# One K tile of the third head split into parts of 64, 48, 8, 4 and 4 partitions

## The chip, the core and the metric

The kernel runs on one core of a Trainium2 chip. The time is the device time of one execution in microseconds (us), lower is better. Before the change it is 177.32 us, the median of three runs (177.17 to 178.05). The core has five instruction streams that matter here: PE (matrix products), DVE (vector work, here mostly 32 x 32 transposes), ACT, POOL, and SP, which in this kernel does nothing but issue transfers. The transfers themselves are carried out by 16 DMA engines. Each transfer is divided among them by rows, each engine works through its own queue in order, and each reports to the transfer's semaphore when its share is done; the transfer is complete when all have.

## The reference

Two rounds of attention and a gated block, each with a residual connection, for four sequences with one new position each:

```python
x = x + _A_ref(_layernorm(x), A_k_cache, A_v_cache, A_wq, A_wo)
x = x + _B_ref(_layernorm(x), B_w_gate, B_w_up, B_w_down)
x = x + _A_ref(_layernorm(x), A_k_cache, A_v_cache, A_wq, A_wo)
x = x + _B_ref(_layernorm(x), B_w_gate, B_w_up, B_w_down)
```

`_A_ref` makes 32 query heads from x, takes the last W = 2048 positions of the K and V caches (8 key heads of width 128, each shared by four query heads), forms softmax(q k / sqrt(128)) v and multiplies by wo. `_B_ref` is (sigmoid(x w_gate) * (x w_up)) w_down with an inner width of 1792. All data are bf16. Both attention rounds read the same caches and weights, with another x.

## The kernel before

All data come through SBUF from HBM. An arena of 50 slots, 4 KB per partition each, holds tiles; most tiles are two slots, 128 partitions of 8 KB, 1 MB. The K tiles of all eight heads take 32 slots and stay from the first round to the second, so K is loaded once. V, wq, wo and the weights of the gated block go through the remaining 18 slots and a side buffer, and most of V and all of wq are loaded a second time for the second round.

One K tile holds one head and two of the four sequences. `pair_d` (line 478) gives its source: for each of 64 row groups p and each of the two sequences b, one run of 32 positions, 8 KB. Row p of sequence b lands in partition 2p + b. `kpair(h, bp)` (line 482) is the tile for head h and sequence pair bp: slots 4h + 2bp and the one after it. `load_k` (line 485) issues the two tiles of a head. Its first three heads (`AHEAD = 3`) are issued at the start, behind the four wq tiles; from there on a list of loads (lines 1478 to 1502) gives the order: K3, wo of the first two heads, V0, K4, V1, K5 and so on. The loads are on SP in exactly that order.

For head h, `k_transpose` (line 885) transposes the four slots in place on DVE: T{h}_0 and T{h}_1 in the two slots of tile (h, 0), T{h}_2 and T{h}_3 in those of tile (h, 1). `softmax_unit` (line 896) then makes the scores on PE (line 918, behind the mask's products at line 907), the maximum on DVE (line 931) and the exponentials on ACT (line 946); `turn_p` (line 957) permutes and transposes the result, `pv_unit` (line 995) multiplies with the two V tiles (line 1009), and `wo_unit` with wo. A V tile's slot goes back to the pool after its products, and the next load that is waiting on SP takes it. The front of head h + 2 is written down ahead of the PV products of head h. The very last weights are the three w_down tiles of the second gated block; their products are line 1428, and a copy (line 1439) and a transfer of 4 KB out end the kernel.

No engine runs the operations in the order in which they are written. Each is noted with an engine, an estimated duration, and the tokens that it reads and writes (`_Plan.op`, line 52); a planner (`_schedule`, line 92) walks all of them with estimated times, transfers included, and gives each engine but SP a fixed order, earliest possible start first. SP keeps the order as written. `_assign_sync` (line 180) then adds the semaphore waits that the tokens require. There are 24 semaphores for transfers; each transfer uses the next, and waits until the transfer 24 places before it has landed.

A token `("slot", n)` stands for one slot; `tok(s)` is the pair of a tile. Everything that reads a slot waits for the last operation that wrote its token.

Of the kernel before, what the change touches and what calls it, by code (L numbers as in the profile page):

```python
# [254 lines left out]
class _SlotPool:  # L255
# [16 lines left out]
    bw_8k=421.0, bw_4k=409.0, bw_3k=405.0, bw_1k=347.0,  # L272
# [6 lines left out]
def build(nc, A_x, A_k, A_v, A_wq, A_wo, B_wg, B_wu, B_wd, out, cfg=None):  # L279
# [29 lines left out]
    AHEAD = 3  # L309
# [15 lines left out]
    with es:  # L325
# [52 lines left out]
        def slot_ap(s):  # L378
            if s == SIDE:
                return side[:, 0:SLOT]  # L380
            return arena[:, s * SLOT:(s + 1) * SLOT]
# [4 lines left out]
        def tile_ap(s):  # L386
            return arena[:, s * SLOT:(s + 2) * SLOT]

        def tok(s):
            return [("slot", s), ("slot", s + 1)]  # L390

        def c_dve(n, rate=None):
            return tm["dve_fix"] + n * (tm["dve_f32"] if rate is None else rate)
# [4 lines left out]
        def dma(name, dst, src, w, r=(), rate="bw_4k", nbytes=None, sem=None):  # L398
            if nbytes is None:
                nbytes = dst.partition_size() * dst.free_nbytes()  # L400
            o = P.op("sync", name, 0.0, lambda e, dst=dst, src=src: e.dma_start(dst, src),  # L401
                     r=r, w=w, dma_bytes=nbytes, dma_rate=tm[rate])
            if sem is not None:
                o.sem = sem
                o.inc = 16
            return o
# [56 lines left out]
        def need(name):  # L463
            while name not in where:
                take_load()
            return where[name]
# [11 lines left out]
        def pair_d(cache, h, bp):  # L478

            return cache[2 * bp:2 * bp + 2, h, SK - W:SK, :].rearrange("b (p j) d -> p b (j d)", p=64)  # L480

        def kpair(h, bp):
            return tile_ap(4 * h + 2 * bp)

        def load_k(h):
            where[("K", h)] = h
            for bp in range(2):
                dma("K%d_%d" % (h, bp), kpair(h, bp), pair_d(A_k, h, bp), w=tok(4 * h + 2 * bp), rate="bw_8k")

        def load_half(name, src, rate, size, where_):  # L490
            left[name] = 1
            homes[name] = [where_]
            on_free[name] = lambda s: hfree.add(s)

            def emit(s):
                dma(str(name), slot_ap(s)[:, 0:size], src, w=stok(s, size), rate=rate)
            loads.append((name, emit))
# [134 lines left out]
        def keep_wq(c):  # L632
            def f(s):
# [13 lines left out]
             r=[("ones_f",)], w=[("e", 0)])  # L647
# [6 lines left out]
        for jh in range(2):  # L654
            for bp in range(2):
                for i in range(2):
# [7 lines left out]
                         r=[("ones_f",), ("e", 0), ("perm",)], w=[("perm", jh, bp, i)])  # L664
# [5 lines left out]
             r=[("ones_f",), ("e", 0)], w=[("msk_s",)])  # L670
        P.op("vector", "msk_s2", 100.0, lambda v: v.tensor_scalar(msk_s[:, :], msk_s[:, :], -1.0e30, None, ALU.mult),
             r=[("msk_s",)], w=[("msk_s",)])
        P.op("gpsimd", "msk_m", 200.0,
             lambda g: g.affine_select(msk_m[:, :], ones_f[:, 0:2], [[-1, 2]], ALU.is_equal, 0.0, base=0, channel_multiplier=1),
             r=[("ones_f",), ("e", 0)], w=[("msk_m",)])
        P.op("vector", "sel_f", 200.0,
             lambda v: v.tensor_reduce(sel_f[:, :], perm[:, :].rearrange("p (g x) -> p x g", x=NR), AXX, ALU.add),
             r=perms + [("e", 0)], w=[("sel_f",)])
        P.op("gpsimd", "sel_b", 200.0, lambda g: g.tensor_copy(sel_b[:, :], sel_f[:, :]),
             r=[("sel_f",), ("e", 0)], w=[("sel_b",)])  # L680
        P.op("vector", "sel_r", 100.0,
             lambda v: v.tensor_reduce(sel_r[:, :], sel_f[:, :].rearrange("p (g y) -> p y g", g=2), AXX, ALU.add),
             r=[("sel_f",), ("e", 0)], w=[("sel_r",)])
        P.op("vector", "eyew", 200.0,
             lambda v: v.tensor_reduce(eyew[:, 96:128], ident.rearrange("p (a j) -> p j a", a=4), AXX, ALU.max),
             r=[("e", 0), ("eyew0",)], w=[("eyew",)])
        P.op("vector", "maskp", 200.0,
             lambda v: v.tensor_reduce(maskp[:, :], ident.rearrange("p (a j) -> p a j", a=4), AXX, ALU.max),
             r=[("e", 0)], w=[("maskp",)])
        P.op("vector", "maskb", 100.0,  # L690
             lambda v: v.tensor_reduce(maskb[:, :], maskp[:, :].rearrange("p (j b) -> p b j", j=2), AXX, ALU.max),
             r=[("maskp",)], w=[("maskb",)])
# [3 lines left out]
             r=[("eyew",)], w=[("maske",)])  # L696
        P.op("vector", "mod4", 100.0,
             lambda v: v.tensor_reduce(mod4[:, :], ey.rearrange("p (e m) -> p m e", m=REP), AXX, ALU.max),
             r=[("eyew",)], w=[("mod4",)])
# [4 lines left out]
             r=[("mod4",), ("maskp",)], w=[("selm",)])  # L704
# [4 lines left out]
             r=[("e", 0)], w=[("permo",)])  # L709
# [4 lines left out]
             r=[("sel_r",)], w=[("maskr",)])  # L714
# [170 lines left out]
        def k_transpose(h):  # L885
            need(("K", h))
            for t in range(4):
                v32 = slot_ap(4 * h + t).bitcast(F32)
                P.op("vector", "T%d_%d" % (h, t), c_dve(1024), lambda v, v32=v32: v.transpose(v32, v32),  # L889
                     r=[("slot", 4 * h + t)], w=[("slot", 4 * h + t)])  # L890

        ucount = [0]

# [314 lines left out]
        def attn_first():  # L1208
            def front(h):
                k_transpose(h)  # L1210
                softmax_unit("0.%d" % h, h)
                turn = lambda: turn_p(0, "0.%d" % h, h % 2, PBS[h % 2])
                return turn
# [265 lines left out]
        for h in range(AHEAD):  # L1479
            loads.append((("K", h), lambda _, h=h: load_k(h)))  # L1480
        for h in range(HKV):
            if h + AHEAD < HKV:
                loads.append((("K", h + AHEAD), lambda _, h=h + AHEAD: load_k(h)))
            if h % 2 == 0 and h + 2 < HKV:
                load_wo(h // 2)
            for bp in range(2):
                load_v(h, bp, 0, 2 if (h, bp) in keep + stay else 1)
# [21 lines left out]
        n = len(P.ops)  # L1509
# [45 lines left out]
def bass_interleave_layers__sliding_block_cached__glu_gated_glu__decode_kernel(  # L1555
    nc, A_x, A_k_cache, A_v_cache, A_wq, A_wo, B_x, B_w_gate, B_w_up, B_w_down, out,
):
    build(nc, A_x, A_k_cache, A_v_cache, A_wq, A_wo, B_w_gate, B_w_up, B_w_down, out)
# [28 lines left out]
```

## Time and profile before

| | |
|---|---|
| median of three runs | 177.32 us (177.17 to 178.05) |
| the profiled execution's own time | 177.11 us |
| its span, first to last instruction | 175.4 us |
| data moved by transfers (queue q1) | 69.74 MB in 12344 packets |
| PE busy | 107.5 us, 61% of the span |
| DVE busy | 104.5 us, 60% |
| K tiles: issue to landing, median | 24.9 us |
| V tiles of 1 MB: issue to landing, median | 16.5 us |

The page of the profile has the DMA engines' mean busy share in tenths for 40 equal slices of the span, the queues with their packets, and the chain of waits that ended last. The queues q8 and q14 are instruction fetches: the engines' programs are read through the same 16 DMA engines as the data. "Chain" lines give the start, the length and what was running or waited for. Time line rows give start, length, engine, line, operation, output and input, shapes and a count, with the idle time just before in brackets and what ended it. Besides these views the trace keeps, for every transfer, the times at which its semaphore was counted up, and for every packet its start, length and size; times read from there are given with the transfer they belong to.

In SP's order the transfers that matter are numbered: 1 to 4 wq, 5 and 6 K0, 7 and 8 K1, 9 and 10 K2, 11 and 12 K3, 13 wo, 14 and 15 V0, and 81 to 83 the last three w_down tiles.

### The profile page before, as it was taken

How to read it: one execution, taken by the hardware profiler on the slowest of the kernel's cores; microseconds unless marked ns; L12 is line 12 of the kernel's file. 1: busy time of each engine (PE TensorE's matmuls, PEld its weight loads, DVE VectorE, ACT ScalarE, POOL GpSimd, SP SyncE). 2: the span in 40 equal slices, each digit the busy share in tenths (PEclk: the TensorE clock that was granted, in tenths of full speed). 3: DMA queues.
4: the chain of work that ended last, by engine and by line, in shares of the span. 5: the costliest groups of instructions: out<-in, count | busy, mean ns of one | idle time of the engine just before them, and what ended most of it. 6: DMA issues, size and time to landing. Idle time of an engine off the chain costs nothing.

```text
span 175.4 us, 3934 instructions
## 1 busy us (share of the span) xinstructions
PE 107.5 (61%) x1663; PEld 55.4 (32%) x1663; DVE 104.5 (60%) x258; ACT 32.7 (19%) x87; POOL 22.1 (13%) x90
## 2 busy tenths in 40 slices
PE   0536246259566273561766456558977999776584
PEld 0203112014334041340445452143222444425432
DVE  6307997994957738378322382315399999733351
ACT  2002021322303003021030000100133455430011
POOL 6100010101101001010010000000011553442000
PEclk9999999999999999999999999999999999965555
DMA  5999999999999999999999999999999999999980
GB/s 177 422 430 428 420 422 422 409 419 420 422 422 409 422 422 422 419 407 424 424 405 423 415 397 406 405 406 403 409 411 404 422 422 422 420 415 419 419 347 28
DMA packets 12370, 70.00 MB, mean 399 GB/s; under 512 B 1336, under 2 KB 1344, under 8 KB 6336
## 3 DMA queue, kind: packets, MB, share of 16 engines
q1 hardware_dynamic: 12344, 69.74, 97.2%
q8 instruction: 13, 0.21, 0.5%
q14 instruction: 5, 0.04, 0.1%
q10 hardware_dynamic: 8, 0.00, 0.0%
HBM read 69.73 MB, written 0.00 MB: 398 GB/s over the span
## 4 chain that ended last, share of the span: by engine, by line
DMA 71%; PE 12%; DVE 8%; SPq 6%; issue 1%; DVEq 0%
DMA arena<-in_A_v_cache_dram 48%; DMA arena<-in_B_w_down_dram 15%; SPq L401 6%; DMA arena<-in_A_wq_dram 4%; DMA arena<-in_B_w_up_dram 4%; PE ps L1009 3%; PE ps L918 2%; PE ps L1092 2%; DVE arena L592 1%; DVE small L931 1%; PE ps L1383 1%; DVE ps L599 1%; PE ps L907 1%; PE ps L959 1%; PE ps L1428 1%
## 5 line engine op out<-in xcount | busy, mean ns | idle before, releaser
L889 DVE STREAM_TRANSPOSE arena<-arena 128x1024 f32<-128x1024 f32 x32 | 37.0, 1204 | 0.1
L1009 PE MATMUL ps<-side,arena 128*128 128x8 bf16 x576 | 18.2, 168 | 13.8 <-DMA arena<-in_A_v_cache_dram 13.8
L918 PE MATMUL ps<-arena,side 128*32 128x512 bf16 x256 | 25.1, 525 | 0.0
L1009 PEld LDWEIGHTS ps<-side,arena 128*128 128x128 bf16 x576 | 16.8, 104 | 20.1 <-DMA arena<-in_A_v_cache_dram 18.4
L931 DVE TENSOR_REDUCE small<-ps 128x1 f32<-128x512 f32 x16 | 10.8, 676 | 17.3 <-PE ps L918 17.2
L946 ACT ACTIVATE side<-ps,small 128x512 bf16<-128x512 f32 x16 | 11.0, 687 | 36.9 <-PE ps L1028 18.4
L907 PE MATMUL ps<-small,msk_s 128*32 128x512 bf16 x64 | 8.6, 526 | 14.1 <-DVE arena L889 13.3
L882 ACT CAST side<-ps 128x256 bf16<-128x256 f32 x16 | 5.9, 371 | 34.3 <-PE ps L918 25.6
L961 ACT CAST side<-ps 128x512 bf16<-128x512 f32 x16 | 9.4, 586 | 10.8 <-PE ps L959 10.8
L918 PEld LDWEIGHTS ps<-arena,side 128*32 128x32 bf16 x256 | 8.1, 119 | 10.2 <-issue 7.2
L975 POOL CAST small<-small 128x1 bf16<-128x1 f32 x9 | 1.7, 187 | 76.2 <-ACT side L946 76.2
L959 PE MATMUL ps<-side,perm 128*128 128x512 bf16 x16 | 8.1, 507 | 5.0 <-ACT side L946 5.0
L830 PE MATMUL ps<-arena,xn 128*4 128x512 bf16 x60 | 7.6, 574 | 3.4 <-DMA arena<-in_A_wq_dram 3.2
L786 ACT ACTIVATE small<-ps 128x4 f32<-128x4 f32 x4 | 0.7, 174 | 48.2 <-PE ps L782 48.2
L1383 PE MATMUL ps<-arena,xn 128*4 128x448 bf16 x60 | 7.0, 550 | 3.1 <-DMA arena<-in_B_w_up_dram 1.5
L1092 PE MATMUL ps<-arena,side 128*32 128x512 bf16 x112 | 8.2, 416 | 0.2 <-DVE small L943 0.2
L966 DVE STREAM_TRANSPOSE side<-side 128x256 f32<-128x256 f32 x16 | 6.9, 432 | 2.2 <-ACT side L961 2.0
L877 PE MATMUL ps<-side,eyew 32*128 32x64 bf16 x64 | 5.6, 217 | 3.3 <-ACT side L882 2.4
L907 PEld LDWEIGHTS ps<-small,msk_s 128*32 128x32 bf16 x64 | 1.7, 98 | 17.0 <-DVE arena L889 15.6
L1018 DVE TENSOR_TENSOR onb<-ps,rinv 128x16 bf16<-128x16 f32 x9 | 1.7, 185 | 9.0 <-PE ps L1009 8.8
L842 DVE STREAM_TRANSPOSE side<-ps 128x512 f32<-128x512 f32 x3 | 2.1, 717 | 7.9 <-PE ps L830 7.8
L1392 DVE STREAM_TRANSPOSE side<-ps 128x448 f32<-128x448 f32 x4 | 2.6, 640 | 7.0 <-PE ps L1383 7.0
(126 smaller groups left out, 139.5 us busy)
## 6 DMA issues: line engine op xcount, KB each, us to landing
arena<-in_A_v_cache_dram SPq DMA_DIRECT2D x26, 1024.0 KB, 16.5
arena<-in_A_k_cache_dram SPq DMA_DIRECT2D x16, 1024.0 KB, 24.9
arena<-in_A_wq_dram SPq DMA_DIRECT2D x4, 1024.0 KB, 7.9
arena<-in_A_wo_dram SPq DMA_DIRECT2D x3, 1024.0 KB, 26.6
arena<-in_A_v_cache_dram SPq DMA_DIRECT2D x6, 512.0 KB, 6.8
arena<-in_A_wq_dram SPq DMA_DIRECT2D x5, 512.0 KB, 6.6
arena<-in_B_w_up_dram SPq DMA_DIRECT2D x4, 448.0 KB, 6.1
arena<-in_B_w_gate_dram SPq DMA_DIRECT2D x2, 896.0 KB, 20.8
```

Of the source, the lines that this page charges most:

```text
L401: o = P.op("sync", name, 0.0, lambda e, dst=dst, src=src: e.dma_start(dst, src), r=r, w=w, dma_bytes=nbytes, dma_rate=tm[rate])
L830: last = pe.matmul(ps[32 * hh:32 * hh + NB, qb, :], xn[:, c * NB:(c + 1) * NB], src[:, o + hh * 512:o + (hh + 1) * 512], start=(c == 0), s ...
L889: P.op("vector", "T%d_%d" % (h, t), c_dve(1024), lambda v, v32=v32: v.transpose(v32, v32), r=[("slot", 4 * h + t)], w=[("slot", 4 * h + t)])
L907: last = pe.matmul(ps[32 * gi:32 * gi + 32, bank, :], msk_s[:, :], msk_m[:, :].unsqueeze(1).broadcast_to([128, 256, 2]), start=True, stop= ...
L918: last = pe.matmul(ps[32 * gi:32 * gi + 32, bank, :], qbd[:, q0:q0 + 32], kt[:, cp // 2, cp % 2, jh * NJ:(jh + 1) * NJ, :], start=False, s ...
L931: lambda v: v.tensor_reduce(nmax[:, k2:k2 + 1], ps[:, bank, :], AXX, ALU.max),
L946: lambda a: a.activation(prow[:, :].rearrange("p (m x t) -> p m x t", x=32, t=2), ps[:, bank, :].rearrange("p (m t x) -> p m x t", x=32, t ...
L959: lambda pe: pe.matmul(ps[:, pb, :], perm[:, :], prow[:, :], start=True, stop=True),
L961: P.op("scalar", "pc" + tag, c_act(512), lambda a: a.copy(prow[:, :], ps[:, pb, :]), r=[("ppb", pb)], w=[("prow",)], banks=(pb,))
L1009: last = pe.matmul(ps[:, ob, bp * 8:bp * 8 + 8], slot_ap(ss[j // NJ])[:, j % NJ * 128:(j % NJ + 1) * 128], ev[:, j % 2, j % 16 // 2, x0:x0 ...
L1092: last = pe.matmul(ps[32 * g:32 * g + 32, ob, :], ew[:, g, mq, t], src.rearrange("p (m t d) -> p t m d", t=2, d=128)[:, t], start=(n == 0) ...
L1383: last = pe.matmul(ps[32 * g:32 * g + NB, gub[n], 0:NF], xn[:, c * NB:(c + 1) * NB], src[:, g * NF:(g + 1) * NF], start=(c == 0), stop=(c ...
```

## The change

The tile of head 2 and sequences 0 and 1 (`CUT = AHEAD - 1 = 2`, bp = 0) is no longer one transfer. Part 0 is all 64 rows of sequence 0 (partitions 0, 2, ..., 126). Part 1 is rows 0 to 47 of sequence 1 (partitions 1, 3, ..., 95). Both stand in the old place. The last 16 rows of sequence 1 follow: rows 48, 50, ..., 62 (partitions 97, 101, ..., 125) behind the other tile of head 2, rows 49, 53, 57, 61 (partitions 99, 107, 115, 123) behind the first tile of head 3, rows 51, 55, 59, 63 (partitions 103, 111, 119, 127) behind its second tile. Part 0 carries the slots' own tokens; parts 1 to 4 have tokens of their own, `("rows", 1)` to `("rows", 4)`, and the transposes T2_0 and T2_1 read all four. SP's order at the start becomes wq, K0, K1, part 0, part 1, K2_1, part 2, K3_0, part 3, K3_1, part 4, wo, V0.

```diff
+        CUT = AHEAD - 1
+
+        def k_rows(n):
+            b, p0, p1, step = ((0, 0, 64, 1), (1, 0, 48, 1), (1, 48, 64, 2), (1, 49, 64, 4), (1, 51, 64, 4))[n]
+            dma("K%dr%d" % (CUT, n), kpair(CUT, 0)[2 * p0 + b:128:2 * step, :] if p1 == 64 else kpair(CUT, 0)[2 * p0 + b:2 * p1:2 * step, :],
+                pair_d(A_k, CUT, 0)[p0:p1:step, b, :], w=[("rows", n)] if n else tok(4 * CUT), rate="bw_8k")
+
         def load_k(h):
             where[("K", h)] = h
             for bp in range(2):
+                if (h, bp) == (CUT, 0):
+                    k_rows(0)
+                    k_rows(1)
+                    continue
                 dma("K%d_%d" % (h, bp), kpair(h, bp), pair_d(A_k, h, bp), w=tok(4 * h + 2 * bp), rate="bw_8k")
+                if h == CUT:
+                    k_rows(2)
+                if h == CUT + 1:
+                    k_rows(3 + bp)
...
                 P.op("vector", "T%d_%d" % (h, t), c_dve(1024), lambda v, v32=v32: v.transpose(v32, v32),
-                     r=[("slot", 4 * h + t)], w=[("slot", 4 * h + t)])
+                     r=[("slot", 4 * h + t)] + ([("rows", n) for n in range(1, 5)] if h == CUT and t < 2 else []),
+                     w=[("slot", 4 * h + t)])
```

## The prediction

> **What bounds the kernel now.** I read the page first, then the chain of waits at its end, then the sixteen completion counts of every transfer in the trace, then the time lines of SP, DVE and PE around 30 us.
>
> ```profile
> DMA  5999999999999999999999999999999999999980
> ...
> q1 hardware_dynamic: 12344, 69.74, 97.2%
> q8 instruction: 13, 0.21, 0.5%
> q14 instruction: 5, 0.04, 0.1%
> ```
>
> The DMA row is 9 from the second slice to the thirty-eighth: the transfers are never out of work as a whole, 69.74 MB in 12344 packets. Beside them run 18 packets that are instructions, not data: 13 of 16 KB and, inside the span, five of 8 KB.
>
> ```profile
> 144.83 27.09 DMA arena<-in_B_w_down_dram
> 171.93 0.04 issue
> 171.97 0.60 PE ps L1428 x16
> 172.57 0.04 issue
> 172.60 0.41 PE ps L1428 x8
> ```
>
> This is the end of the chain. The transfer issued at 144.83 lands at 171.93, 27 us later, since that much is queued ahead of it. PE works 0.60 us on it, and then on the last one, which landed at 172.56. So the end of the kernel is the moment when the last transfer is complete, and a transfer is complete when the slowest of its 16 DMA engines is.
>
> How far the engines lie apart is in the trace's completion counts. Transfer 11 in SP's order (K3_0) counts from 30.28 to 30.51. At 30.75 a 16 KB instruction packet begins on one engine. Transfer 12 (K3_1) then has fifteen counts from 32.76 to 33.02 and the sixteenth at 34.31: that engine is 1.3 us late, and it stays late, because each engine works through a queue of its own. The next 16 KB packets (47.3, 59.0, 75.6, 88.0, 95.5, 103.0, 118.4 us) each make another engine late by about as much; those from 132.2 on hit engines already late. The last transfer's counts are five at 170.00 to 170.28, seven from 170.96 to 171.66, and four at 172.40, 172.41, 172.44 and 172.56: the four that were hit twice. Twelve engines wait up to 2.5 us for four.
>
> **Which engines are the late ones.** A packet of 8 KB begins 306 ns after the one before it on its engine, so up to 30 us each engine can be followed by its phase. Eight engines begin wq at 1.83 to 1.95 us, the other eight at 2.50 to 2.63. The four rows of x, a transfer of four partitions, went to four of the first eight: two of its completions (1.886 and 1.947) are followed 6 ns later by the first wq packets at 1.892 and 1.953. The 16 KB packet at 30.752 follows a packet begun at 30.445 on the engine that began at 2.517: one of the second eight. Phases of the second, fourth and fifth hit suit second-group engines too, though a phase alone does not tell neighbours apart. I take the eight that fetch to be the second group. [...]
>
> **The change, part by part.** Removed: one transfer of 128 rows of 8 KB, eight rows on each engine (its 16 counts lie within 0.24 us). Added: 64 rows (four each), 48 rows (three each), then 8, 4 and 4 rows, which by the example of x go one each to eight, four and four engines of the first group. So the second group carries 7 rows for K2_0 in place of 8, the first four 4+3+1+1+1 = 10, the other four 8. Bytes are the same.
>
> - The late engines: one row less, 306 ns. They show no gap: where the fast ones starved at transfer 66 (first counts 129.12 and 131.84, 2.72 us apart, against 2.48 usual) the late ones went 130.70 to 133.17, 2.47. So -0.31 us at their end, from 172.56 to 172.25.
> - The first four: two rows more, +0.61. If they are among the five at 170.28 or before, they end at 170.9. In the worst placing one is the engine at 171.66; it ends at 172.27. Either way the last count comes 0.29 to 0.31 earlier.
> - Four more completion packets: 6 ns each by the phases, so 0.02 us. I take nothing.
> - Four more issues on SP. The nearest rows are 0.33 and 0.64 us each, so 1.3 to 2.6 us of SP, ahead of K2_1, K3_0, K3_1, wo0 and the V tiles:
>
> ```profile
> 2.88 5.99 SPq L401 DMA_DIRECT2D arena<-in_A_k_cache_dram  x8
> 8.91 2.10 SPq L401 DMA_DIRECT2D arena<-in_A_wo_dram  x1
> 11.05 6.45 SPq L401 DMA_DIRECT2D arena<-in_A_v_cache_dram  x2
> ...
> SPq L401 <- PE ps L1009: 29.7, 8, 8.0
> ```
>
> The first two rows show issues growing from 0.6 us to 2.1, the third over 3: SP is already held by full queues, ten transfers (25 us) ahead of the engines. What it loses is hidden there, and later it waits up to 8.0 us for a slot with no gap in the DMA row. Cost zero; without that cover 1.3 to 2.6 us.
> - Two transposes now wait for parts 1 to 4. Part 4 comes behind K3_1 and lands on the first group at about 33.0 + 0.6 = 33.6 us, not 25.6.
>
> ```profile
> 27.32 1.18 DVE L889 STREAM_TRANSPOSE arena<-arena 128x1024 f32<-128x1024 f32 x1
> 29.36 0.69 DVE L931 TENSOR_REDUCE small<-ps 128x1 f32<-128x512 f32 x1 [0.86 <-PE ps L918]
> ...
> 30.87 2.33 DVE L889 STREAM_TRANSPOSE arena<-arena 128x1024 f32<-128x1024 f32 x2
> ...
> 33.59 3.43 DVE L889 STREAM_TRANSPOSE arena<-arena 128x1024 f32<-128x1024 f32 x3
> ...
> 34.84 0.62 PE L907 MATMUL ps<-small,msk_s 128*32 128x512 bf16 x4 [1.72 <-DVE arena L889]
> ...
> 39.38 1.01 PE L1009 MATMUL ps<-side,arena 128*128 128x8 bf16 x32 [1.35 <-DMA arena<-in_A_v_cache_dram]
> ```
>
> Counting L889 from head 0, the one at 27.32 is T2_0, the pair at 30.87 T2_1 and T2_2, and 33.59 begins with T2_3. With T2_2 and T2_3 ahead (K2_1 lands at 28.1) and T3_0 (K3_0, 30.5) in the gap, T2_0 and T2_1 run from 33.6 to 35.9, and S2, queued on PE behind them, starts 1.1 us later. PE sits idle 1.35 us before the first PV, which waits for V anyway: the 1.1 fits. If the planner also puts T3_1 first, it is 2.3 us and the first PV is 1 us late; its slot is returned 1 us late to an SP that is 25 us ahead. Zero; 1 to 2 us if SP were not ahead.
> - Rows with a step of two or four partitions: no row shows such a transfer. Bounds: at best a row takes 306 ns as ever. At worst two engines get in each other's way all through both large parts and the seven rows take twice as long: 7 x 306 = +2.14 us. I take the first, since K tiles, whose source has a split 64 x 2, and wq, whose source has not, take the same 2.48 us per MB. The range keeps the other end.
>
> Sum: -0.31 us, on the profiled execution's 177.11 (span 175.4 and 1.7 around it) 176.8; that execution lies 0.21 under the median of the runs, 177.32, and on the median the sum gives 177.0. That is -0.17%, less than the 0.5% that a measurement of this kernel can tell from no change.
>
> **Rivals.**
>
> *The split rows collide* (slower). Place: the two large parts, about 18 to 25 us, ahead of everything late in the program. [...] If pairs share one way into SBUF, the 64-row part alone costs up to 4 x 306 = 1.22 us, both 2.14. It decides as soon as the loss on a late engine passes the 0.31 won, and nothing hides it, since late engines never idle: 177.32 - 0.31 + 1.22 = 178.2, at most 179.2. For it: engines work at a constant 306 ns per row, as something saturated would. Against it: no pair of rows shows two engines at half pace. [...] Chance 0.2.
>
> *Rows move, ports do not* (no gain). The parts' last rows lie in the upper partitions; if the late engines are held up while others write there, they give back the 306 ns: 177.3. So it would be, too, if the end hung on compute: the chain passes over PE and DVE from 116 to 144.8. Against that stand 27 us from issue to landing. Chance 0.14.
>
> *The late engines are the ones loaded.* Then +0.61: 177.9, within 0.5% still. The first hit's phase speaks against it. Chance 0.06.
>
> *The wait for part 4 bites* through another order of the planner's queue: 1 to 2 us if the 25 us of cover did not hold, 178.3 to 179.3. Chance 0.03.
>
> *More than one row is won*, if shifted phases let some fetch fall where an engine starves: 1.3 us per hit, 176.0. Chance 0.04.
>
> **How the numbers follow.** Forecast 0.53, the rivals as given. The predicted time is the forecast's, 177.0; its own range is 176.6 to 177.4, for the runs before spread from 177.11 up. To hold 8 in 10 the range goes to 178.5, over the cheaper half of the collision, and to 176.5 below. Faster by over 0.5% (under 176.4): 0.05, the last rival and a little noise. Slower (over 178.2): the larger part of the collision and the late wait, 0.19. The rest, 0.76, lies within.
>
> **What would show it.** Right: the last transfer's four late counts about 0.3 us earlier, all else at the end alike; K3_1 and the V tiles each complete 0.3 us earlier on the late engine; the four-row parts with four counts only. The split is wrong if the two large parts take more than 2.2 us together, the cover if DVE or PE idles longer before the first PV and the DMA row breaks. A last landing at 172.56 or later refutes the sum.

## The result, and the profile after

The changed kernel takes 178.39 us, the median of 11 runs (177.93 to 179.88); the kernel before, beside it, 177.16 us (11 runs, 176.91 to 178.05). The ratio is 1.0071, with a 95% interval of 1.0052 to 1.0091: slower by 1.2 us, where 177.0 was forecast. The profiled execution took 177.93 us with a span of 176.2, against 177.11 and 175.4. It is the fastest of the eleven, 0.46 under their median, so what its trace accounts for is somewhat less than the 1.2 us.

The page after, its DMA rows and the queues:

```profile
DMA  4999999999999999999999999999999999999990
GB/s 187 428 426 424 424 365 394 365 427 415 422 415 416 421 418 424 420 410 421 420 411 422 414 398 406 402 407 400 409 417 411 422 424 418 413 423 423 417 374 35
...
q1 hardware_dynamic: 12376, 69.74, 97.2%
q8 instruction: 13, 0.21, 0.5%
q14 instruction: 5, 0.04, 0.1%
```

The same GB/s row of the kernel before:

```profile
GB/s 177 422 430 428 420 422 422 409 419 420 422 422 409 422 422 422 419 407 424 424 405 423 415 397 406 405 406 403 409 411 404 422 422 422 420 415 419 419 347 28
```

The DMA row is as full as before, the bytes are the same 69.74 MB, and the packets are 32 more (16 + 16 + 8 + 4 + 4 completions for the five parts in place of 16). What differs is in slices 6, 7 and 8 (22 to 35 us): 365, 394 and 365 GB/s in place of 422, 422 and 409. They are 57, 28 and 44 GB/s short, in slices of 4.4 us: 0.57 MB, or 1.35 us at 420 GB/s. From the ninth slice to the thirty-eighth none is short by more than 7. These are the slices in which the five parts and the whole tiles between them land. In windows of 2 us there (columns: the stretch, its length, the busy time of PE, PEld, DVE, ACT and POOL, the granted clock, the share of the DMA engines' time in packets, GB/s), first before, then after:

```profile
24.00:26.00 2.00, 0.46 (x1) 0.10 (x1) 1.93 (x5) 0.78 (x2) 0.36 (x2) 1.00 1.00 418
...
28.00:30.00 2.00, 1.52 (x20) 0.37 (x8) 1.14 (x2) 0.37 (x1) 0.00 (x0) 1.00 1.00 418
30.00:32.00 2.00, 0.36 (x5) 0.12 (x2) 1.86 (x6) 0.78 (x2) 0.17 (x1) 1.00 1.01 410
```

```profile
24.00:26.00 2.00, 0.00 (x0) 0.10 (x1) 1.93 (x5) 0.78 (x2) 0.38 (x3) 1.00 0.93 291
26.00:28.00 2.00, 1.35 (x15) 0.61 (x19) 1.31 (x3) 0.58 (x1) 0.37 (x2) 1.00 1.08 426
28.00:30.00 2.00, 1.52 (x16) 0.39 (x8) 1.49 (x2) 0.37 (x1) 0.00 (x0) 1.00 0.95 360
30.00:32.00 2.00, 0.09 (x2) 0.00 (x0) 1.86 (x6) 0.74 (x2) 0.00 (x0) 1.00 1.01 373
```

From 24 to 26 us, where the 48 rows come, the engines are still 0.93 busy but move 291 GB/s: they are not short of work, their packets last longer (lengths below). After parts 0 and 1 the rate is 426 again, as before, and around parts 2 and 3 it falls once more, less deeply (360 and 373).

The trace's completion counts give the loss part by part. The table has the mean of a transfer's counts in us since the mean of K1_1's, and what the parts account for. "Rows alone" takes 0.306 us for each row per engine that was not yet loaded, and otherwise the pace of before:

```
                before   after   rows alone, from the entry above   loss
K2_1             4.96     5.37    4.96 - 0.31 = 4.65                +0.72   (64 and 48 rows ahead of it)
K3_0             7.45     8.24    5.37 + 2.49 + 0.15 = 8.01         +0.22   (8 rows ahead of it)
K3_1            10.02    11.11    8.24 + 2.57 + 0.08 = 10.89        +0.23   (4 rows)
wo0             12.62    13.95    11.11 + 2.60 + 0.08 = 13.79       +0.16   (4 rows)
in all                                                              +1.33
```

The end of the chain of waits, after:

```profile
171.25 0.54 DVE side L1408
171.82 0.23 DVE rinv L1430
172.05 0.14 issue
172.18 1.31 PE ps L1444 x48
173.51 0.31 PE ps L1444 x8
```

Of the last transfer's 16 counts the last came at 173.47 (before: 172.56), and the last eight matmuls follow at 173.51. The chain is drawn here through the computation instead, since by the profile its 48 matmuls end at 173.49, 0.02 after that count. But the ends of matmuls are modelled, and the starts say otherwise. By the records of the single matmuls, the last eight start 0.04 after the last count, as they did before (172.56, then 172.60), and 0.24 after the four matmuls issued ahead of them at 173.27, where the groups of four before that follow each other 0.06 to 0.11 apart. So the last landing still sets the end.

The same line of the time line before:

```profile
170.80 2.19 PE L1428 MATMUL ps<-arena,rinv 128*4 128x128 bf16 x56 [0.67 <-DMA arena<-in_B_w_down_dram]
```

The computation is now close behind. Its first matmul on this line began at 172.18, 1.38 later than before (170.80; there too it began 0.14 after the vector operation that makes rinv, which ended at 170.66), and the last landing came only 0.91 later, so the computation used up 0.47 of its slack and has some 0.1 to 0.2 left. Followed back, it waits for a wq transfer of the second round that landed at 124.44, 1.40 later than before (123.05): it hangs on transfers too. That both paths are late from the transfers between 22 and 35 us is the likeliest reading, since from the ninth slice on the GB/s row hardly falls short again before its end.

### The profile page after: what moved, and what is told of

It reads as the page before. It is cut to its first block, busy times and chain, and to the rows that moved or that the text cites. A ratio compares the mean times of both kernels' runs of the same rounds, so it can differ in the third digit from the quotient of the medians.

```text
span 176.2 us, 3929 instructions
## 1 busy us (share of the span) xinstructions
PE 102.3 (58%) x1651; PEld 55.6 (32%) x1663; DVE 104.7 (59%) x258; ACT 32.7 (19%) x87; POOL 22.1 (13%) x90
## 3 DMA queue, kind: packets, MB, share of 16 engines
q1 hardware_dynamic: 12376, 69.74, 97.2%
## 4 chain that ended last, share of the span: by engine, by line
DMA 55%; DVE 19%; PE 14%; SPq 7%; issue 3%; POOL 1%; ACT 1%; POOLq 0%; DVEq 0%
DMA arena<-in_A_v_cache_dram 48%; SPq L401 7%; DMA arena<-in_A_wq_dram 4%; DMA arena<-in_B_w_up_dram 3%; PE ps L1025 3%; DVE small L947 3%; DVE arena L1117 3%; PE ps L1399 2%; DVE arena L1122 2%; PE ps L1108 2%; DVE side L982 1%; DVE arena L607 1%; DVE small L951 1%; PE ps L934 1%; DVE side L955 1%
## 5 line engine op out<-in xcount | busy, mean ns | idle before, releaser
L892 PEld LDWEIGHTS ps<-side,eyew 32*128 32x128 bf16 x64 | 3.3, 106 | 8.6 <-ACT side L897 5.4
```

Of the source, the lines that this page charges most:

```text
L892: last = pe.matmul(dst[:, :, a * REP:(a + 1) * REP], eyew[32 * hh:32 * hh + 32, 96 - 32 * a:224 - 32 * a], src, start=True, stop=True)
```

## The experiments

All five-part kernels use one helper, with the parts as a tuple (sequence, first row, end, step). "In place" means that the parts stand together where the tile stood, with no whole transfer between them. Packet lengths below are those of 8 KB packets, by the trace's records, median (longest) in ns, in three stretches. The kernel before is the first row:

```
                          24-26 us    27.6-28.6    30.6-31.6
before                    313 (321)   312 (321)    311 (318)
changed kernel            393 (635)   436 (553)    379 (506)
64 + 64                   311 (321)   312          312
64 + 48 + 16, in place    527 (614)
halves                    589 (622)
five parts, in place      507 (681)
small parts elsewhere     454 (613)   311 (320)    348 (498)
64+32+16+8+8, in place    552 (699)
64 + 32 + 32, in place    311 (318)   309          309
```

**One step of two alone: even rows, then odd rows.** Is the 64-row part the costly one, as the collision rival had it?

```diff
+        ROWS = ((0, 0, 64, 1), (1, 0, 64, 1))
```

> The tile as 64 even and 64 odd rows, both in the old place, nothing small, nothing late. Collision (rows of a stepped transfer reach SBUF by ways that other engines also use): packets of both parts take 450 to 630 ns in place of 309, the next K tile is complete at 28.7 to 29.0 us in place of 28.03, the end 0.7 to 1.0 us late. Cost per added transfer (1.23 us over four of them): 0.3 us. Late wait of the transposes alone: no loss. Rows moved between engines alone: no loss.

Measured: 177.25 against 177.22, ratio 1.0003 [0.9991, 1.0015]. Windows from the even and odd parts:

```profile
22.00:24.00 2.00, 1.52 (x16) 0.38 (x8) 1.82 (x3) 0.37 (x1) 0.00 (x0) 1.00 1.04 430
24.00:26.00 2.00, 0.36 (x2) 0.10 (x1) 1.90 (x6) 0.78 (x2) 0.26 (x2) 1.00 0.99 414
```

No dip, and from 22 to 26 us no packet over 321 ns. A part of 64 rows with a step of two costs nothing here, and neither does cutting the tile in two in this way.

**The cut by columns.** Two parts of 128 partitions and 4 KB each, so that every row stays on its partition.

```diff
+                    for n in range(2):
+                        dma("K%dc%d" % (h, n), kpair(h, 0)[:, n * SLOT:(n + 1) * SLOT], pair_d(A_k, h, 0)[:, :, n * SLOT:(n + 1) * SLOT],
+                            w=[("slot", 4 * h + n)], rate="bw_8k")
```

> The tile as two transfers of 128 partitions by 4 KB, left and right half. Collision: none, since every row goes the way it goes in a whole tile; next K tile complete at 28.0, end unchanged within 0.1 us. Cost per added transfer: 0.3 us. Late wait: no loss.

Measured: 177.77, ratio 1.0033 [1.0001, 1.0064]. The loss is all in the first half:

```profile
22.00:24.00 2.00, 1.40 (x16) 0.34 (x8) 1.81 (x4) 0.37 (x1) 0.00 (x0) 1.00 0.96 301
24.00:26.00 2.00, 0.48 (x1) 0.10 (x1) 1.93 (x5) 0.78 (x2) 0.38 (x2) 1.00 1.05 436
```

301 GB/s, with packets of 4 KB that last up to 549 ns, then 436 in the second half. The interval only just leaves out no change, but the trace shows the loss too: it is 0.33 us on the mean engine by the counts. This run was meant as a control with no collision in it, and as that it is a miss: packets grew longer though every row went to its usual partition. That a row also takes the way it takes in a whole tile was the author's assumption; no record shows it. The cause stays open. Rows of 4 KB alone are not it, since the two V halves of the kernel before, 4 KB rows as well, land 1.28 and 1.27 us after the transfer ahead of them, as the second half does here (1.27; the first takes 1.54).

**The 48 rows, in place.**

```diff
+        ROWS = ((0, 0, 64, 1), (1, 0, 48, 1), (1, 48, 64, 1))
```

> 64, 48 and 16 rows, all in the old place: eight rows per engine, as before. Collision: all three parts slow, next K tile complete at 28.7 to 29.1, end 0.7 to 1.1 us late. If it is the 8, 4 and 4 rows on few engines that cost: no loss here. Cost per added transfer: 0.6 us. Late wait: no loss.

Measured: 178.46, ratio 1.0068 [1.0051, 1.0085].

```profile
24.00:26.00 2.00, 0.36 (x2) 0.10 (x1) 1.90 (x6) 0.78 (x2) 0.24 (x2) 1.00 1.03 250
26.00:28.00 2.00, 1.42 (x16) 0.52 (x19) 2.00 (x4) 0.59 (x1) 0.52 (x3) 1.00 0.98 385
```

K2_1 is complete at 29.28, against 28.03. The run has 12376 packets, 32 more than before: 16 completions for each of the three parts. So in equal shares every engine gets 4 + 3 + 1 rows, the tile's old eight, none is relieved and none loaded, and no transfer stands between the parts. It still loses as much as the changed kernel: the loss comes from the parts themselves, not from the rows moved between engines nor from the tiles between the parts.

**The lower and the upper half.** The strongest form of the collision: 64 rows at once, on partitions 0 to 63.

```diff
+                    for n in range(2):
+                        dma("K%dh%d" % (h, n), kpair(h, 0)[64 * n:64 * n + 64, :], pair_d(A_k, h, 0)[32 * n:32 * n + 32, :, :],
+                            w=[("half2",)] if n else tok(4 * h), rate="bw_8k")
```

> Partitions 0 to 63 as one transfer, 64 to 127 as another, no step. Collision by shared ways into SBUF: if 64 neighbouring partitions are reached by half of the ways, each part takes twice its time, the next K tile is complete at 30.5 in place of 28.03 and the end is 2.4 us late. If instead a step between partitions is what is slow: no loss. Cost per added transfer: 0.3 us.

Measured: 179.9, ratio 1.0157 [1.0141, 1.0173].

```profile
22.00:24.00 2.00, 1.52 (x16) 0.39 (x8) 1.83 (x3) 0.37 (x1) 0.00 (x0) 1.00 1.07 229
24.00:26.00 2.00, 0.36 (x1) 0.10 (x1) 1.90 (x6) 0.78 (x2) 0.27 (x2) 1.00 1.03 229
26.00:28.00 2.00, 1.42 (x16) 0.55 (x19) 1.49 (x3) 0.59 (x1) 0.49 (x3) 1.00 0.98 209
```

With 64 rows as in the first experiment, only on other partitions, the rate is 209 to 229 GB/s instead of 414 to 430, at a DMA share of 0.98 to 1.07. Packets take 604 ns (median from 24 to 28 us): an engine moves 8192 B in that time, 13.6 GB/s, against the 26.8 of 306 ns. So with all rows of a part on one half the engines work at half pace here; what they share, no record shows.

**All five parts in place**, with the changed kernel's rows:

```diff
+                    for n in (0, 1, 2, 3, 4):
+                        k_rows(n)
```

> The five parts of the change, all in the old place, one after the other. If the 48 rows and the small parts collide (even and odd 64 did not): the loss stays, the next K tile complete 1.0 to 1.4 us later than before (28.03), end 0.9 to 1.3 us late, about the same as the change. If the wait of the two transposes behind other tiles is what costs: no loss, 177.2. If the fall comes from interrupting whole tiles with small parts: about half the loss, 177.8.

Measured: 178.09, ratio 1.0055 [1.0036, 1.0073], which overlaps with the changed kernel's 1.0052 to 1.0091.

```profile
24.00:26.00 2.00, 0.36 (x2) 0.10 (x1) 1.90 (x6) 0.78 (x2) 0.24 (x2) 1.00 0.95 234
26.00:28.00 2.00, 1.42 (x16) 0.52 (x19) 1.52 (x3) 0.59 (x1) 0.52 (x3) 1.00 0.97 287
```

The transfers between the parts are not what costs, and they save nothing that can be told apart.

**The small parts on other partitions.** The 48 rows are now rows 16 to 63, and the small parts come from rows 0 to 15, on partitions 1 to 31. The numbers of rows and the places in the queue are the changed kernel's.

```diff
+        ROWS = ((0, 0, 64, 1), (1, 16, 64, 1), (1, 0, 16, 2), (1, 1, 16, 4), (1, 3, 16, 4))
```

> [...] Collision: the 48 rows still take 450 to 630 ns each (next K tile 0.4 to 0.6 us late); the small parts no longer slow the other eight engines, so the tile behind each comes 2.48 us after the one before on these; end 0.3 to 0.7 us late in place of 1.2. If a small part costs by being short, wherever it lands: the same as the change, 178.4.

Measured: 177.88, ratio 1.0035 [1.0022, 1.0048].

```profile
24.00:26.00 2.00, 0.46 (x1) 0.10 (x1) 1.93 (x5) 0.78 (x2) 0.36 (x2) 1.00 0.94 279
...
28.00:30.00 2.00, 1.52 (x20) 0.37 (x8) 1.64 (x2) 0.37 (x1) 0.00 (x0) 1.00 1.01 422
30.00:32.00 2.00, 0.23 (x5) 0.07 (x2) 1.86 (x6) 0.78 (x2) 0.04 (x1) 1.00 1.02 385
```

Around the 8 rows the rate is 422 instead of 360 and no packet lasts over 320 ns (553 in the changed kernel). Parts 1 to 4 lose 0.63, 0.04, 0.12 and 0.10 us here, 0.89 in all. The choice of rows, and with it of partitions, turns a part of 8 rows that costs 0.22 us into one that costs 0.04. The parts of 4 rows are not free here either: around part 3 packets last up to 498 ns (506 in the changed kernel). The 48 rows cost about as much as before (0.63 against 0.72).

**The late wait alone.** The kernel before, with T2_0 and T2_1 waiting for K3_1:

```diff
-                     r=[("slot", 4 * h + t)], w=[("slot", 4 * h + t)])
+                     r=[("slot", 4 * h + t)] + ([("slot", 4 * h + 6)] if h == AHEAD - 1 and t < 2 else []),
+                     w=[("slot", 4 * h + t)])
```

> The kernel before, whole tiles, but transposes T2_0 and T2_1 also wait for the second tile of head 3, as they do in the change for part 4. Collision: no loss of time, 177.2, the transfers as before; PE and DVE idle 1 to 2 us more around 34 to 40 us. If the late wait is what costs: 1.2 us late.

Measured: 177.13, ratio 0.999 [0.997, 1.0009]. The time line of PE:

```profile
37.21 0.62 PE L908 MATMUL ps<-small,msk_s 128*32 128x512 bf16 x4 [3.97 <-DVE arena L889]
37.61 1.93 PE L919 MATMUL ps<-arena,side 128*32 128x512 bf16 x16
40.01 0.39 PE L877 MATMUL ps<-side,eyew 32*128 32x64 bf16 x4 [0.48 <-ACT side L882]
40.33 1.01 PE L1010 MATMUL ps<-side,arena 128*128 128x8 bf16 x32
```

S2 starts at 37.21 instead of 34.84, after 3.97 us of idle PE, and the first PV at 40.33 instead of 39.38. It costs nothing at the end. The reason foreseen was that SP's transfers are far enough ahead.

**Halving the rows on and on, in place.** The parts have 64, 32, 16, 8 and 8 rows. Is it the odd number of 48, three rows per engine, or the spread?

```diff
+        ROWS = ((0, 0, 64, 1), (1, 0, 64, 2), (1, 1, 64, 4), (1, 3, 64, 8), (1, 7, 64, 8))
```

> [...] If only a count like 48, which does not spread as a whole tile does, collides: the 32 and 16 rows take 309 ns each, the late engines win their 0.3 us, 176.9. If every part whose rows reach engines other than the usual ones collides: the 16 and 8 rows take 450 ns and more, end 0.3 to 0.8 us late.

Measured: 177.98, ratio 1.0049 [1.0027, 1.0071], with 270 GB/s from 24 to 26 us:

```profile
24.00:26.00 2.00, 0.56 (x1) 0.10 (x1) 1.93 (x5) 0.78 (x2) 0.40 (x3) 1.00 1.06 270
```

This tile collides though no part gives an engine three rows (12392 packets: 16, 16, 16, 8 and 8 completions in place of 16). By the next run it is the parts of 16 (partitions 3, 11, ..., 123), 8 and 8 rows together that do it; the run does not tell them apart.

**The same without the parts of 16 and 8 rows.**

```diff
+        ROWS = ((0, 0, 64, 1), (1, 0, 64, 2), (1, 1, 64, 2))
```

> 64 even rows, then the odd ones as 32 at partitions 1, 5, ..., 125 and 32 at 3, 7, ..., 127, all in place: each spreads over the tile as a whole tile does, and engines carry eight rows each. Collision only where engines leave their usual partitions: packets stay at 309 to 325 ns, next K tile complete at 28.0 to 28.2, 177.2. If three parts, or a step of four partitions, cost by themselves: 0.3 us or more late.

Measured: 177.17, ratio 0.9992 [0.9973, 1.0011].

```profile
24.00:26.00 2.00, 0.40 (x1) 0.10 (x1) 1.90 (x6) 0.78 (x2) 0.31 (x2) 1.00 1.03 430
```

Three parts, 32 rows with a step of four among them, at 430 GB/s, and from 22 to 26 us no packet over 321 ns. Cutting the tile in three costs nothing that can be told, and neither do a step of four and the extra completions. Against the run before it, that leaves the parts of 16, 8 and 8 rows.

**Two rows per engine less.** What is a row off every engine worth at the end? The last 32 rows of the tile are left out and are zeros, so the run serves for its time alone.

```diff
+        ROWS = ((0, 0, 64, 1), (1, 0, 64, 2))
```

> Leaves out 32 odd rows of the tile (partitions 3, 7, ..., 127), which are zeros from a memset on DVE near the start; 64 even and 32 odd rows are loaded, six per engine in place of eight. If the end is the late engines' work, every row taken from them is worth 306 ns: 0.6 us earlier, 176.6. If the end hangs on compute, or the rows are made up for elsewhere: 177.2.

Measured: 176.56 against 177.26, ratio 0.9961 [0.9939, 0.9983]: 0.70 us less, where two rows are 2 x 0.306 = 0.61.

```profile
146.19 25.75 DMA arena<-in_B_w_down_dram
171.94 0.04 issue
171.99 0.41 PE ps L1447 x8
```

The last landing is 171.94, 0.62 before the 172.56. What engines save at 24 us reaches the end in full. Since all sixteen save it here, the run does not tell the late engines from the others.

## Why the prediction was wrong

**The step that failed** is "Rows with a step of two or four partitions: no row shows such a transfer", bounded by 0 and +2.14 us and taken at 0. It is +1.33 us on the mean engine: +0.72 over the two large parts, put down to the 48 rows since 64 alone cost nothing, and +0.22, +0.23 and +0.16 for the small parts. The reason given for 0 was that K tiles and wq, with and without a split source, take the same 2.48 us. But both are whole tiles of 128 partitions, and neither row says anything of a part that goes to some of them. The range was right to keep the other end; the value should have been taken from inside it, for seven rows were to go where no row of the profile had been.

The prediction's own signs of being wrong came in: the two large parts took 2.85 us (22.82 to 25.67 by the means of their counts), over its 2.2, and the last landing was later than 172.56.

**The other terms.** With the loss put in for the zero, the last landing should be 172.56 - 0.31 (a row less on the late engines) + 1.33 - 0.13 (the transfers of the profiled run before the change's place were that much earlier) = 173.45; it was 173.47. For the run with the small parts elsewhere the same sum is 172.56 - 0.31 + 0.89 - 0.06 = 173.08, and 173.10 was measured. Agreement that close is luck: for the first experiment, whose K3 tiles lose nothing, the sum gives 172.51, and 172.87 was measured. No run shows the -0.31, for none shows which engines take the 8, 4 and 4 rows; what the trace of the changed kernel shows is eight, four and four counts for these parts, and a last landing 0.91 later. Taken without the row won, the sum is later than the last landing by 0.29 us for the changed kernel, 0.39 for its five parts in place and 0.29 for the small parts elsewhere, and earlier by 0.26 for 64 + 32 + 16 + 8 + 8; in these four the late engines would have a row less, by the author's assumption that all parts of 8 and 4 rows go to the other eight. For the other kernels it is earlier by 0.02 to 0.40. So three of the four speak for the row won, but only as a term that a sum needs, and the sum takes the loss to be the same on late engines as on the mean. The late wait alone was measured to be free (177.13), and for the four SP issues no run shows a cost at the end, though V0 was issued at 13.02 instead of 11.05 and PE waited 4.13 us ahead of S2. S2 began 2.68 us later than before (37.52 against 34.84), not 1.1. In the changed kernel V0 itself is what the first PV waits for: it landed at 40.81, and PE went on at 40.85.

```profile
37.52 0.62 PE L923 MATMUL ps<-small,msk_s 128*32 128x512 bf16 x4 [4.13 <-DVE arena L904]
...
40.85 1.02 PE L1025 MATMUL ps<-side,arena 128*128 128x8 bf16 x32
```

Part 4's four counts came at 34.84 to 34.92, not at the estimated 33.6, which had no loss in it. The 8-row part's semaphore counted eight with data, the 4-row parts' four each, as for x.

**The rivals.** *The split rows collide* was right in its sign, and engines at half pace were measured (604 ns in the halves against 306), though no run shows that pairs of them share a way into SBUF. It was wrong in its place, so that its size (178.2, against 178.39) came close by luck. It put the whole price on the two large parts, the 64 rows alone at up to 1.22 us. They cost nothing when they stand by themselves (ratio 1.0003). The 48 rows, behind them, cost 0.72, and the small parts, which it did not price, 0.61. *Rows move, ports do not* (the ports of its name no record shows) had a reason that fits the small parts: a row taken off an engine is still written to the same partition, and at each small part the packets lasted longer, up to 553 ns around the 8 rows. But it stopped at giving back 0.31, and which engine held up which was not shown. If its reading is right the two rivals are one, and the price went past the gain because the whole tiles lost again at each small part (0.22, 0.23 and 0.16 us). *The late engines are the ones loaded* has no longer packets in it and gives no rate of 291 GB/s; with its +0.61 in place of the -0.31 the sum above would be 174.37, not 173.47. *The wait for part 4 bites* and *more than one row is won* did not happen.

**What makes a part collide.** In these runs two kinds of part were clean, both spread over all partitions: 64 rows, the even or the odd ones (packets up to 321 ns from 22 to 26 us), and 32 with a step of four (up to 321). Longer packets, from 24 to 26 us, came with 64 rows on one half (median 589), with 48 on the lower three quarters (527 with the 16 rows behind them) or on the upper (454), and with 16, 8 and 8 rows together (552); these are spread too, the 16 with a step of eight, so an even spread was not enough there. A part of 8 rows was clean on partitions 1 to 29 (packets up to 320 ns), and not on 97 to 125 (up to 553). That is shown as a comparison of runs, and the half pace on one half by the halves. Two things stay open. Which engine took which row, no record shows. And row p of a sequence always lands in partition 2p + b, so each of these runs also changed the places in HBM that a part is read from; that the partitions count and not the source is a reading that no run separates, and the cut by columns shows that packets can grow longer with all partitions in their place.

## What to carry to other kernels

In this kernel, whose DMA row is full, the thing to look at was not only how many packets each engine has but also which rows, and with them which partitions, a part is made of: a part of 8 rows cost 0.22 us on partitions 97 to 125 and 0.04 on 1 to 29. The split into 64, 48, 8, 4 and 4 rows, made to move rows to other engines, cost 1.33 us, for a gain estimated at 0.31. This tile could be cut for nothing into even and odd rows (ratio 1.0003), and into 64, 32 and 32 with a step of four in the smaller two (0.9992). And when no row of a profile shows a kind of transfer, agreement between two rows of another kind is no reason to take the lower bound.

## What had not been expected

- A full DMA row hides such a loss: the share stays at 0.93 to 1.08 while the rate falls from 418 to 291 GB/s, and with the halves to 209. The rate, not the share, shows it.
- Two halves of a tile are free as even and odd partitions (177.25) and cost 2.7 us as partitions 0 to 63 and 64 to 127 (179.9 against 177.22).
- Two halves by columns, with all partitions in their place, cost 0.55 us in the first half alone (packets of 4 KB up to 549 ns), for a reason that these runs do not show. Its interval, 1.0001 to 1.0064, only just leaves out no change.
